# The opening of an FFT and gated MLP kernel: order of its transfers, z tiles of two chunks, the first weight quarter ahead of x

## The chip, the cores and the metric

The kernel runs on one core of one Trainium2 chip. The metric is device time in microseconds (us) of one execution; lower is better.

## The reference

x has the shape (8, 3008, 256): 8 batches of 3008 rows. The output has 24064 rows of 256 columns. All is fp32. Cut to what matters:

```python
X = np.fft.fft(np.fft.fft(x, axis=1), axis=2).real      # the transform
h = X.reshape(8 * 3008, 256) @ w_in                     # 256 -> 2048
g = h * np.cos(h)
out = g @ w_out                                         # 2048 -> 256
```

## The kernel before

**The transform.** A column of 3008 = 47 * 64 values is transformed in two halves. The first half (`first_half`) multiplies chunks of x by a constant L; its results are called z. The second half (`second_half`) multiplies z by a constant BJ, after z has been turned around: each chunk's z is copied from PSUM to SBUF by ScalarE (`keep_z`), stored to a scratch tensor in HBM (`store_z`, tensor zd), and loaded back in another layout (`load_z`, tile z). The transform along the 256 columns is not made on x: it is folded into the weights. `weights(e, n)` multiplies quarter n of moe_w_in (512 of 2048 columns) by the constant CS, with e = 0 for WC (cosine) and e = 1 for WS (sine); `keep_weights` copies the product to SBUF, and `fold_weights` does both. Row 0 of WS is used on its own: `take_wn(0)` turns it into per-partition scalars wn by four tiny products, and for the other quarters `send_wn(n)` stores the row to HBM (tensor wd) and `load_wn(n)` loads it back as a column of wn. GpSimd clears the row after that.

**Batches, chunks, groups.** A batch has 32 pairs of x rows' residues, cut into 8 chunks of 4 (`first_half(b, c)`, c = 0 to 7). x is loaded in 4 pieces of two chunks each (`load_x(b, p)`): four transfers for a piece, and six for piece 0. `fold(b, c, e)` prepares a chunk (VectorE and GpSimd for batch 0, GpSimd later). The second half has 6 groups (`second_half(b, g)`), each of 225 or 256 columns of tokens.

**The main loop.** For each batch and group there are 8 steps, one for each pair of feature blocks, and each step has two half-steps; k counts the half-steps over all. In a half-step TensorE multiplies the group by WC and WS (`mm1`, line 550), ScalarE and VectorE compute h * cos(h) (lines 562 to 592), GpSimd forms sums (line 608), and TensorE multiplies by moe_w_out and combinations of it (`mm2`, line 641; the combinations come from `combine_w2` on GpSimd). `seed` (line 531) writes the start value of an `mm1` sum and needs the wn column of that feature block, so quarter n of wn is wanted from k = 4 n - 1 on. The transform of batch b + 1 is spread over the loop of batch b (`transform`).

**The opening** is the code ahead of the loop: the transform of batch 0 as far as the first group, the first weights, and all loads of constants. Its order is written out by hand, and every engine works through its own instructions in that order. Transfers are issued by SP (`nc.sync`), except for some by ScalarE (`nc.scalar`). `keep_busy` runs products whose results nobody reads. In the opening each `store_z` stores the part of z that group 0 needs (j 0 to 4); the rest (j 4 to 24) is stored and loaded later.

**Order before.** SP's list: L, piece 0 of x, CS, weight quarter 0, pieces 1 to 3 of x, weight quarter 1, a piece of BJ (line 207), weight quarter 2; then the stores of z chunk by chunk, the loads of z, the first part of moe_w_out, weight quarter 3, and so on. Chunks 4 to 7 are stored by ScalarE. TensorE: first halves 0 and 1, the weights of quarter 0, first halves 2 to 7, three more weight products (quarter 1 twice, quarter 2 once), the second half of group 0, `keep_busy`, the loop. The remaining three weight products are made in the loop's first half-steps (`pw`, line 893 and 930).

Buffers: z chunks lie in tiles of 512 columns; tags "zs" (4 buffers) and, for chunks 4 to 7 of batch 0, "pq". The raw weight quarters 0 to 2 lie in two tiles under the tags "mr" and "cb", quarter 3 under "r"; these tags are used otherwise in the loop.

Of the kernel before, what the change touches and what calls it, by code (L numbers as in the profile page):

```python
# [114 lines left out]
def kernel(  # L115
# [30 lines left out]
    def load_x(b, p):  # L146
        if (b, p) not in xs:
            take_x(b, p)
        xt = xs[b, p]
        xv = xt.rearrange("r (i d) -> r i d", d=ND)  # L150
        i0 = XP * p
        for r0, r1, at, by in ((0, 32, 0, 3), (31, 47, 2, 6)):
            lo, hi = xv[at:NX:by], xv[at + by // 2 : NX : by]
            nc.sync.dma_start(out=lo, in_=x_r[b, r0:r1, i0 : i0 + XP, :])  # L154
            if p == 0:
                nc.sync.dma_start(out=hi[:, 0:1], in_=x_r[b, r0:r1, 32:33, :])  # L156
                nc.sync.dma_start(  # L157
                    out=hi[:, 1:XP], in_=x_r[b, r0:r1, 63 : 64 - XP : -1, :]
                )
            else:  # L160
                nc.sync.dma_start(
                    out=hi, in_=x_r[b, r0:r1, 64 - i0 : 64 - i0 - XP : -1, :]
                )
# [3 lines left out]
    wr = [spool.tile([128, 7 * 256], FP, tag=tag, bufs=1, name="wr") for tag in ("mr", "cb")]  # L167
    wl = spool.tile([128, 1024], FP, tag="r", bufs=4, name="wr")

    def raw(q, i):  # L170
        return wl[:, 512 * i : 512 * i + 512] if q == 3 else wr[i][:, 512 * q : 512 * q + 512]
# [5 lines left out]
    def load_cs():  # L177
        for i in range(2):
            nc.sync.dma_start(out=CS[i], in_=CS_dr.ap()[i * 128 : (i + 1) * 128, :])

    def load_w(q):
        for i in range(2):
            nc.sync.dma_start(
                out=raw(q, i),
                in_=moe_w_in[i * 128 : (i + 1) * 128, 512 * q : 512 * q + 512],
            )
# [12 lines left out]

    nc.sync.dma_start(out=L, in_=L_dr.ap())  # L200
    load_x(0, 0)
    load_cs()
    load_w(0)
    for p in (1, 2, 3):
        load_x(0, p)
    load_w(1)
    load_bj(0, 512)
    load_w(2)
# [51 lines left out]
    zss = {}  # L260

# [36 lines left out]
    def keep_z(b, c, pz):  # L298
        tag, n = ("zs", 4) if b or c < 4 else ("pq", 8)
        zs = spool.tile([128, 512], FP, tag=tag, bufs=n, name="zs")  # L300
        nc.scalar.copy(out=zs, in_=pz)
        zss[b, c] = zs
# [32 lines left out]
    def store_z(b, c, j0=0, j1=NJ, eng=nc.sync):  # L335
        half, q = divmod(c, NCH // 2)
        if q == 0 and j0 == 0:
            zds[b, half] = dpool.tile([32, 2 * NJ * 128], FP, tag="zd", bufs=4, name="zd")
        zd, zs = zds[b, half], zss[b, c]
        for e in range(2):  # L340
            p0 = 16 * e + IP * q
            eng.dma_start(
                out=zd[p0 : p0 + IP, 256 * j0 : 256 * j1].rearrange("i (y d) -> y i d", d=128),
                in_=zs[64 * e + 2 * j0 : 64 * e + 2 * j1, :].rearrange("y (i d) -> y i d", d=128),
            )

    def load_z(b, half, j0=0, j1=NJ):
        if b not in z2s:
            z2s[b] = spool.tile([128, NJ * 128], FP, tag="z2", bufs=1, name="z2")
        for r in range(2):  # L350
            p0 = 64 * half + 32 * r
            nc.sync.dma_start(
                out=z2s[b][p0 : p0 + 32, 128 * j0 : 128 * j1].rearrange("i (j d) -> i j d", d=128),
                in_=zds[b, half].rearrange("i (j r d) -> r i j d", r=2, d=128)[r, :, j0:j1],
            )
# [48 lines left out]
    def transform(b):  # L404
# [5 lines left out]
        for p in range(4):  # L410
# [5 lines left out]
            for c in (2 * p, 2 * p + 1):  # L416
                at(8 * p + 12, store_z, b, c)
# [9 lines left out]
    def fold_weights(e, n, tag="M"):  # L427
        keep_weights(e, n, weights(e, n, tag))

    def weights(e, n, tag="M"):  # L430
        pw = psum("pw", tag)
        for i in range(2):
# [351 lines left out]
    def chunk(c):  # L784
        fold(0, c, 0)
        fold(0, c, 1)

    keep_busy(2, "H", 512)
    keep_busy(2, "H", 512)
    chunk(0)  # L790
    chunk(1)
    first_half(0, 0)
    chunk(2)
    first_half(0, 1)
# [3 lines left out]
    store_z(0, 0, 0, 4)  # L798
    store_z(0, 1, 0, 4)
    chunk(3)  # L800
    first_half(0, 2)
    chunk(4)
    first_half(0, 3)
    store_z(0, 2, 0, 4)
    store_z(0, 3, 0, 4)
    chunk(5)
    first_half(0, 4)
    chunk(6)
    first_half(0, 5)
    store_z(0, 4, 0, 4, nc.scalar)  # L810
    store_z(0, 5, 0, 4, nc.scalar)
    load_z(0, 0, 0, 4)
    chunk(7)
    first_half(0, 6)
    store_z(0, 6, 0, 4, nc.scalar)
    first_half(0, 7)
    store_z(0, 7, 0, 4, nc.scalar)
    load_z(0, 1, 0, 4)
    fold_weights(1, 1)
    send_wn(1)  # L820
    fold_weights(0, 1)
    fold_weights(1, 2)
    send_wn(2)
    load_w2(0, 2)
    load_w(3)
    load_w2(2, 4)
    load_wn(1)
    load_wn(2)
    for c in range(8):
        store_z(0, c, 4)  # L830
# [39 lines left out]
    keep_busy(2, "M", 256)  # L870
    steps[0].pq, steps[0].nb = ready[0, 0]
    for k in range(2 * n + LAG):
# [5 lines left out]
        if cur:  # L878
# [13 lines left out]
            if k == 0:  # L892
                pw = [weights(1, 3)]
# [50 lines left out]
        if k in (1, 2, 3):  # L944
            e, q = ((1, 3), (0, 3), (0, 2))[k - 1]
            keep_weights(e, q, pw[k - 1], nc.vector.tensor_copy)
# [49 lines left out]
```

## Time and profile before

| what | value |
|---|---|
| median of 3 runs | 1946.1 us (1945.9 to 1946.29) |
| profiled execution | 1945.75 us |
| its span, first to last instruction | 1944.0 us |
| TensorE (PE) busy | 1934.2 us, 99% of the span |
| share of PE in the chain that ended last | 98% |
| first product of the main loop (line 550) | starts at 32.30 us |
| transfers | 89.10 MB, mean 46 GB/s; 12.78 MB of it in the first 60 us, 213 GB/s |

All engines run beside each other. PE is the matrix unit, PEld its weight loads, DVE is VectorE, ACT is ScalarE, POOL is GpSimd, SP issues transfers. A time in the trace is counted from the first instruction. An fp32 product shows as two passes on PE, so a count of x4 is two products. The chain that ended last is followed from the last instruction back to whatever released each step. "Idle before" an instruction is the time for which its engine did nothing, and the name behind the arrow is what ended that.

### The profile page before, as it was taken

The page shows a single profiled execution, that of the slowest core. Times are in us where ns is not written, and L with a number is a line of the kernel's source. Part 1 is how long each engine was busy: PE and PEld are TensorE (multiplying, and loading weights), DVE is VectorE, ACT ScalarE, POOL GpSimd, SP SyncE. Part 2 cuts the span into 40 slices and gives each one's busy share as a digit, 9 for nine tenths or more (in the row PEclk, how much of TensorE's full clock was granted, in tenths as well). Part 3 has the DMA queues.
Part 4 walks back from the last instruction along what each step waited for, and adds up shares of the span by engine and source line. Part 5 has one row for each costly group of instructions (what it writes and reads, how often), then busy time and mean ns, then how long its engine had stood idle before and what let it go on. Part 6 is the DMA issues. An engine that isn't in the chain of part 4 may idle for free.

```text
span 1944.0 us, 29626 instructions
## 1 busy us (share of the span) xinstructions
PE 1934.2 (99%) x9234; PEld 1681.9 (87%) x9234; DVE 1459.2 (75%) x2532; ACT 1508.4 (78%) x3444; POOL 1398.0 (72%) x1594
## 2 busy tenths in 40 slices
PE   9999999999999999999999999999999999999998
PEld 5888898888988889888898888988889888898887
DVE  4777777777777777777777777777777777788787
ACT  4777778777787787878778787788777887778775
POOL 3777767786677766787668776677767777666765
PEclk9999999999999999999999999999999999999999
DMA  7511122021220223111130111311013111100001
GB/s 201 129 29 39 35 53 71 18 40 40 57 58 18 42 43 80 32 24 40 40 90 21 39 25 41 88 24 40 22 42 88 24 39 28 39 23 16 11 14 31
DMA packets 178494, 89.10 MB, mean 46 GB/s; under 512 B 104945, under 2 KB 175391, under 8 KB 176674
## 3 DMA queue, kind: packets, MB, share of 16 engines
q1 hardware_dynamic: 176636, 86.68, 19.2%
q8 instruction: 75, 1.23, 0.3%
q10 hardware_dynamic: 1702, 0.53, 0.1%
q14 instruction: 81, 0.66, 0.1%
HBM read 49.90 MB, written 37.28 MB: 45 GB/s over the span
## 4 chain that ended last, share of the span: by engine, by line
PE 98%; DMA 1%; SPq 0%; DVE 0%; ACT 0%; issue 0%; POOL 0%; POOLq 0%; DVEq 0%
PE M L641 58%; PE H L550 33%; PE pz L275 3%; PE pb L366 2%; DMA wn<-wd 1%; DMA xp<-in_x_dram 1%; PE pw L433 1%; PE pz L272 0%; SPq L154 0%; PE pm L323 0%; DVE r L582 0%; ACT r L588 0%; DVE cb L709 0%; SPq L157 0%; SPq L156 0%
## 5 line engine op out<-in xcount | busy, mean ns | idle before, releaser
L608 POOL TENSOR_TENSOR S<-r 128x512 f32<-128x512 f32 (+1 forms) x383 | 475.0, 1240 | 445.5 <-DVE r L592 396.6
L582 DVE SCALAR_TENSOR_TENSOR r<-r,H 128x512 f32<-128x512 f32 (+1 forms) x768 | 518.8, 675 | 194.6 <-ACT r L578 167.9
L588 ACT ACTIVATE r<-r 128x512 f32<-128x512 f32 (+1 forms) x768 | 477.0, 621 | 240.5 <-DVE r L582 235.6
L592 DVE SCALAR_TENSOR_TENSOR r<-H,r 128x512 f32<-128x512 f32 (+1 forms) x768 | 519.1, 676 | 131.1 <-ACT r L588 90.6
L641 PE MATMUL M<-S,VX 128*128 128x256 f32 (+1 forms) x2304 | 615.2, 376 | 0.0
L641 PEld LDWEIGHTS M<-S,VX 128*128 128x128 f32 x2304 | 435.4, 190 | 71.3 <-issue 22.7
L550 PE MATMUL H<-pq,WC 128*128 128x256 f32 (+1 forms) x1536 | 453.4, 377 | 0.4 <-ACT H L531 0.3
L550 PE MATMUL H<-pq,WS 128*128 128x256 f32 (+1 forms) x1536 | 451.1, 375 | 0.5 <-ACT ew L562 0.5
L578 ACT ACTIVATE r<-H 128x512 f32<-128x512 f32 (+1 forms) x768 | 447.7, 583 | 0.2 <-DVE H L566 0.2
L566 DVE TENSOR_TENSOR H<-ew,H 128x256 f32<-128x256 f32 (+1 forms) x768 | 324.8, 423 | 140.3 <-PE H L550 81.3
L641 PE MATMUL M<-r,w 128*128 128x256 f32 (+1 forms) x1536 | 387.7, 375 | 0.0
L562 ACT ACTIVATE ew<-H 128x256 f32<-128x256 f32 (+1 forms) x768 | 287.8, 375 | 120.2 <-PE H L550 115.9
L531 ACT ACTIVATE H<-nb,wn 128x256 f32<-128x256 f32 (+1 forms) x766 | 366.0, 478 | 2.3 <-DMA wn<-wd 1.4
L641 PEld LDWEIGHTS M<-r,w 128*128 128x128 f32 x1536 | 300.4, 196 | 27.1 <-DVE mr L666 0.2
L550 PEld LDWEIGHTS H<-pq,WS 128*128 128x128 f32 x1536 | 289.9, 190 | 34.5 <-issue 1.0
L550 PEld LDWEIGHTS H<-pq,WC 128*128 128x128 f32 x1536 | 279.2, 190 | 44.6 <-ACT H L531 9.3
L614 POOL TENSOR_TENSOR S<-S,r 128x256 f32<-128x256 f32 (+1 forms) x383 | 275.5, 719 | 30.0
L615 POOL TENSOR_TENSOR S<-r,S 128x256 f32<-128x256 f32 (+1 forms) x383 | 274.5, 717 | 30.0
L641 PE MATMUL M<-S,w 128*128 128x256 f32 (+1 forms) x768 | 225.2, 375 | 0.0
L641 PE MATMUL M<-r,VX 128*128 128x256 f32 (+1 forms) x768 | 225.1, 375 | 0.0
L641 PEld LDWEIGHTS M<-S,w 128*128 128x128 f32 x768 | 150.4, 196 | 14.6
L641 PEld LDWEIGHTS M<-r,VX 128*128 128x128 f32 x768 | 145.8, 190 | 14.6
(78 smaller groups left out, 918.3 us busy)
## 6 DMA issues: line engine op xcount, KB each, us to landing
out_dram<-ob SPq DMA_DIRECT2D x724, 32.0 KB
xp<-in_x_dram SPq DMA_DIRECT2D x56, 256.0 KB
zd<-zs SPq DMA_DIRECT2D x112, 96.0 KB
z<-zd SPq DMA_DIRECT2D x28, 384.0 KB
xp<-in_x_dram SPq DMA_DIRECT2D x56, 128.0 KB
nb<-nd SPq DMA_DIRECT2D x39, 128.0 KB
wr<-in_moe_w_in_dram SPq DMA_DIRECT2D x8, 256.0 KB
w<-in_moe_w_out_dram SPq DMA_DIRECT2D x4, 512.0 KB
```

The source lines that it names most:

```text
L531: nc.scalar.activation(out=h.H[:, 0:T], in_=s.nb[:, 0:T], func=AF.Copy, bias=0.25, scale=wn[:, f : f + 1])
L550: nc.tensor.matmul(h.H[:, 0:T], lhsT=W[:, 128 * f : 128 * f + 128], rhs=s.pq[:, e * T : e * T + T], start=False, stop=True, skip_group_che ...
L562: nc.scalar.mul(out=h.ew[:, 0:T], in_=h.H[:, 0:T], mul=2.0)
L566: nc.vector.tensor_tensor(out=h.H[:, T : 2 * T][:, ::-1], in0=h.ew[:, 0:T], in1=h.H[:, 0:T], op=ALU.subtract)
L578: nc.scalar.activation(out=r, in_=y, func=AF.Copy, bias=BIG, scale=1.0)
L582: nc.vector.scalar_tensor_tensor(out=r, in0=r, scalar=-BIG, in1=y, op0=ALU.add, op1=ALU.subtract)
L588: nc.scalar.activation(out=r, in_=r, func=AF.Sin, bias=0.0, scale=SIN_SCALE)
L592: nc.vector.scalar_tensor_tensor(out=r, in0=y, scalar=-0.25, in1=r, op0=ALU.add, op1=ALU.mult)
L608: tt(out=sv[:, 0:2], in0=qv[:, 1:2].to_broadcast([128, 2, T]), in1=qv[:, 0:4:3], op=ALU.subtract,)
L614: tt(out=sv[:, 2], in0=sv[:, 1], in1=gv[:, 0, 0], op=ALU.subtract)
L615: tt(out=sv[:, 3], in0=gv[:, 1, 0], in1=sv[:, 2], op=ALU.add)
L641: nc.tensor.matmul(acc[key][m // 2][:, 256 * (m % 2) : 256 * (m % 2) + T], lhsT=w, rhs=a, start=first, stop=s.fp == 7, skip_group_check=True,)
```

## The change

It touches the opening and the tiles of z:

- CS and weight quarter 0 are loaded first, half by SP and half by ScalarE. Then comes piece 1 of x (its second halves by ScalarE), then L, then pieces 0, 2 and 3.
- Weight quarters 1, 2 and 3 are one transfer each in place of two.
- z is kept in tiles of two chunks (1024 columns), and one `store_z` stores two chunks: half as many stores, in all batches. In batch 0 the z tiles of chunks 4 to 7 take buffers of x.
- TensorE begins with shorter `keep_busy` products, then the weights of quarter 0, then the first halves of chunks 2, 3, 0, 1, 4 to 7.
- Weight quarters 1 to 3 and the first part of moe_w_out are issued between the stores of z and ahead of the first load of z. The last store and the last load of the opening are split between SP and ScalarE.
- The three weight products ahead of the loop are copied by VectorE, not ScalarE.
- The `keep_busy` between the second half of group 0 and the loop gives way to the first half of a weight product of quarter 3; its second half stays in the loop's half-step 0.

```diff
--- before.py
+++ after.py
@@ -143,7 +143,7 @@
     def take_x(b, p):
         xs[b, p] = spool.tile([128, XP * ND], FP, tag="xp", bufs=4, name="xp")
 
-    def load_x(b, p):
+    def load_x(b, p, other=nc.sync):
         if (b, p) not in xs:
             take_x(b, p)
         xt = xs[b, p]
@@ -153,37 +153,42 @@
             lo, hi = xv[at:NX:by], xv[at + by // 2 : NX : by]
             nc.sync.dma_start(out=lo, in_=x_r[b, r0:r1, i0 : i0 + XP, :])
             if p == 0:
-                nc.sync.dma_start(out=hi[:, 0:1], in_=x_r[b, r0:r1, 32:33, :])
-                nc.sync.dma_start(
+                other.dma_start(
                     out=hi[:, 1:XP], in_=x_r[b, r0:r1, 63 : 64 - XP : -1, :]
                 )
+                other.dma_start(out=hi[:, 0:1], in_=x_r[b, r0:r1, 32:33, :])
             else:
-                nc.sync.dma_start(
+                other.dma_start(
                     out=hi, in_=x_r[b, r0:r1, 64 - i0 : 64 - i0 - XP : -1, :]
                 )
 
 
     CS = [cpool.tile([128, 256], FP, tag=f"CS{i}", name=f"CS{i}") for i in range(2)]
-    wr = [spool.tile([128, 7 * 256], FP, tag=tag, bufs=1, name="wr") for tag in ("mr", "cb")]
-    wl = spool.tile([128, 1024], FP, tag="r", bufs=4, name="wr")
+    wr = {
+        q: spool.tile([128, n], FP, tag=tag, bufs=m, name="wr")
+        for q, tag, n, m in ((0, "r", 1024, 4), (1, "mr", 1792, 1), (2, "cb", 1792, 1), (3, "r", 1024, 4))
+    }
 
     def raw(q, i):
-        return wl[:, 512 * i : 512 * i + 512] if q == 3 else wr[i][:, 512 * q : 512 * q + 512]
+        return wr[q][:, 512 * i : 512 * i + 512]
 
     L = cpool.tile([128, 256], FP, tag="L", name="L")
     BJ = cpool.tile([128, NJ * 128], FP, tag="BJ", name="BJ")
     w2 = cpool.tile([128, 16 * ND], FP, tag="w2", name="w2")
 
-    def load_cs():
-        for i in range(2):
-            nc.sync.dma_start(out=CS[i], in_=CS_dr.ap()[i * 128 : (i + 1) * 128, :])
+    def load_first():
+        for tiles, src, c0, c1 in (
+            (CS, CS_dr.ap(), 0, 256),
+            ([raw(0, i) for i in range(2)], moe_w_in, 0, 512),
+        ):
+            for i, eng in enumerate((nc.sync, nc.scalar)):
+                eng.dma_start(out=tiles[i], in_=src[i * 128 : (i + 1) * 128, c0:c1])
 
     def load_w(q):
-        for i in range(2):
-            nc.sync.dma_start(
-                out=raw(q, i),
-                in_=moe_w_in[i * 128 : (i + 1) * 128, 512 * q : 512 * q + 512],
-            )
+        nc.sync.dma_start(
+            out=wr[q][:, 0:1024].rearrange("p (i f) -> p i f", i=2),
+            in_=moe_w_in[:, 512 * q : 512 * q + 512].rearrange("(i p) f -> p i f", p=128),
+        )
 
     def load_bj(c0, c1):
         nc.sync.dma_start(out=BJ[:, c0:c1], in_=B_dr.ap()[:, c0:c1])
@@ -197,15 +202,11 @@
             in_=moe_w_out.rearrange("(q p) c -> p q c", p=128)[:, 2 * f0 : 2 * f1],
         )
 
+    load_first()
+    load_x(0, 1, nc.scalar)
     nc.sync.dma_start(out=L, in_=L_dr.ap())
-    load_x(0, 0)
-    load_cs()
-    load_w(0)
-    for p in (1, 2, 3):
+    for p in (0, 2, 3):
         load_x(0, p)
-    load_w(1)
-    load_bj(0, 512)
-    load_w(2)
     WC = cpool.tile([128, NDFF], FP, tag="WC", name="WC")
     WS = cpool.tile([128, NDFF], FP, tag="WS", name="WS")
     wn = cpool.tile([128, 16], FP, tag="wn", name="wn")
@@ -258,6 +259,7 @@
                 nc.gpsimd.tensor_copy(**ends)
 
     zss = {}
+    zps = {}
 
     def first_half(b, c, pz=None):
 
@@ -296,10 +298,14 @@
         keep_z(b, c, pz)
 
     def keep_z(b, c, pz):
-        tag, n = ("zs", 4) if b or c < 4 else ("pq", 8)
-        zs = spool.tile([128, 512], FP, tag=tag, bufs=n, name="zs")
-        nc.scalar.copy(out=zs, in_=pz)
-        zss[b, c] = zs
+        p, q = divmod(c, 2)
+        if (b, p) not in zps:
+            if b == 0 and p > 1:
+                zps[b, p] = spool.tile([128, XP * ND], FP, tag="xp", bufs=4, name="zs")
+            else:
+                zps[b, p] = spool.tile([128, 1024], FP, tag="zs", bufs=2, name="zs")
+        zss[b, c] = zps[b, p][:, 512 * q : 512 * q + 512]
+        nc.scalar.copy(out=zss[b, c], in_=pz)
 
     def patch_z(b, c):
         small.append(
@@ -332,24 +338,24 @@
     zds = {}
     z2s = {}
 
-    def store_z(b, c, j0=0, j1=NJ, eng=nc.sync):
-        half, q = divmod(c, NCH // 2)
-        if q == 0 and j0 == 0:
+    def store_z(b, p, j0=0, j1=NJ, engs=(nc.sync, nc.sync)):
+        half, q = divmod(p, 2)
+        if (b, half) not in zds:
             zds[b, half] = dpool.tile([32, 2 * NJ * 128], FP, tag="zd", bufs=4, name="zd")
-        zd, zs = zds[b, half], zss[b, c]
+        zd, zs = zds[b, half], zps[b, p][:, 0:1024]
         for e in range(2):
-            p0 = 16 * e + IP * q
-            eng.dma_start(
-                out=zd[p0 : p0 + IP, 256 * j0 : 256 * j1].rearrange("i (y d) -> y i d", d=128),
+            p0 = 16 * e + XP * q
+            engs[e].dma_start(
+                out=zd[p0 : p0 + XP, 256 * j0 : 256 * j1].rearrange("i (y d) -> y i d", d=128),
                 in_=zs[64 * e + 2 * j0 : 64 * e + 2 * j1, :].rearrange("y (i d) -> y i d", d=128),
             )
 
-    def load_z(b, half, j0=0, j1=NJ):
+    def load_z(b, half, j0=0, j1=NJ, engs=(nc.sync, nc.sync)):
         if b not in z2s:
             z2s[b] = spool.tile([128, NJ * 128], FP, tag="z2", bufs=1, name="z2")
         for r in range(2):
             p0 = 64 * half + 32 * r
-            nc.sync.dma_start(
+            engs[r].dma_start(
                 out=z2s[b][p0 : p0 + 32, 128 * j0 : 128 * j1].rearrange("i (j d) -> i j d", d=128),
                 in_=zds[b, half].rearrange("i (j r d) -> r i j d", r=2, d=128)[r, :, j0:j1],
             )
@@ -413,8 +419,7 @@
             for k in range(4):
                 at(8 * p + (6, 7, 9, 10)[k], fold, b, 2 * p + k // 2, k % 2)
             pairs[per * (b - 1) + 8 * p + 12] = b, 2 * p
-            for c in (2 * p, 2 * p + 1):
-                at(8 * p + 12, store_z, b, c)
+            at(8 * p + 12, store_z, b, p)
         middles.add(per * (b - 1) + 11)
         at(23, load_z, b, 0)
         at(39, load_z, b, 1)
@@ -424,12 +429,12 @@
 
 
 
-    def fold_weights(e, n, tag="M"):
-        keep_weights(e, n, weights(e, n, tag))
-
-    def weights(e, n, tag="M"):
-        pw = psum("pw", tag)
-        for i in range(2):
+    def fold_weights(e, n, tag="M", copy=nc.scalar.copy):
+        keep_weights(e, n, weights(e, n, tag), copy)
+
+    def weights(e, n, tag="M", pw=None, both=(0, 1)):
+        pw = pw or psum("pw", tag)
+        for i in both:
             nc.tensor.matmul(
                 pw,
                 lhsT=CS[i][:, 128 * e : 128 * e + 128],
@@ -785,49 +790,44 @@
         fold(0, c, 0)
         fold(0, c, 1)
 
-    keep_busy(2, "H", 512)
-    keep_busy(2, "H", 512)
-    chunk(0)
-    chunk(1)
-    first_half(0, 0)
-    chunk(2)
-    first_half(0, 1)
+    both = nc.sync, nc.scalar
+    copy_v = nc.vector.tensor_copy
+    keep_busy(1, "H", 512)
+    keep_busy(1, "H", 512)
+    keep_busy(1, "M", 128)
     fold_weights(1, 0, "H")
     fold_weights(0, 0, "H")
     take_wn(0)
-    store_z(0, 0, 0, 4)
-    store_z(0, 1, 0, 4)
-    chunk(3)
-    first_half(0, 2)
-    chunk(4)
-    first_half(0, 3)
-    store_z(0, 2, 0, 4)
-    store_z(0, 3, 0, 4)
-    chunk(5)
-    first_half(0, 4)
-    chunk(6)
-    first_half(0, 5)
-    store_z(0, 4, 0, 4, nc.scalar)
-    store_z(0, 5, 0, 4, nc.scalar)
+    for p in (1, 0):
+        for c in (2 * p, 2 * p + 1):
+            chunk(c)
+            first_half(0, c)
+        store_z(0, p, 0, 4)
+        if p:
+            load_w(1)
+            load_bj(0, 512)
+    load_w(2)
+    load_w(3)
+    load_w2(0, 2)
     load_z(0, 0, 0, 4)
-    chunk(7)
-    first_half(0, 6)
-    store_z(0, 6, 0, 4, nc.scalar)
-    first_half(0, 7)
-    store_z(0, 7, 0, 4, nc.scalar)
-    load_z(0, 1, 0, 4)
-    fold_weights(1, 1)
+    for p in (2, 3):
+        for c in (2 * p, 2 * p + 1):
+            chunk(c)
+            first_half(0, c)
+        store_z(0, p, 0, 4, both if p == 3 else (nc.sync, nc.sync))
+    load_z(0, 1, 0, 4, both)
+    fold_weights(1, 1, "M", copy_v)
     send_wn(1)
-    fold_weights(0, 1)
-    fold_weights(1, 2)
+    fold_weights(0, 1, "M", copy_v)
+    fold_weights(1, 2, "M", copy_v)
     send_wn(2)
-    load_w2(0, 2)
-    load_w(3)
     load_w2(2, 4)
+    store_z(0, 1, 4)
+    store_z(0, 0, 4)
     load_wn(1)
     load_wn(2)
-    for c in range(8):
-        store_z(0, c, 4)
+    store_z(0, 2, 4)
+    store_z(0, 3, 4)
     load_bj(512, 1024)
     for half in range(2):
         load_z(0, half, 4)
@@ -867,7 +867,7 @@
         h.H = psum("H", "H")
         nc.vector.memset(h.H[:, 0 : h.s.T], 0.25)
     second_half(0, 0)
-    keep_busy(2, "M", 256)
+    pw = [weights(1, 3, both=(0,))]
     steps[0].pq, steps[0].nb = ready[0, 0]
     for k in range(2 * n + LAG):
         t, u = divmod(k, 2)
@@ -890,7 +890,7 @@
             if k < AHEAD - 1:
                 mm1(cur, 1)
             if k == 0:
-                pw = [weights(1, 3)]
+                weights(1, 3, pw=pw[0], both=(1,))
         pair = None if u else pairs.pop(t, None)
         if pair:
             b, c = pair
@@ -943,7 +943,7 @@
             dve_h(cur)
         if k in (1, 2, 3):
             e, q = ((1, 3), (0, 3), (0, 2))[k - 1]
-            keep_weights(e, q, pw[k - 1], nc.vector.tensor_copy)
+            keep_weights(e, q, pw[k - 1], copy_v)
         if k == 3:
             send_wn(3)
         elif k == 6:
```

## The prediction

> **What bounds the kernel now.** I read the page first: the shares of the engines and of the chain that ended last.
>
> ```profile
> span 1944.0 us, 29626 instructions
> PE 1934.2 (99%) x9234; PEld 1681.9 (87%) x9234; DVE 1459.2 (75%) x2532; ACT 1508.4 (78%) x3444; POOL 1398.0 (72%) x1594
> PE 98%; DMA 1%; SPq 0%; DVE 0%; ACT 0%; issue 0%; POOL 0%; POOLq 0%; DVEq 0%
> ```
>
> PE is the chain, except in the opening. The change adds no PE work after the opening, so it can only move the moment at which the loop starts, take PE work out of the loop's start, or close gaps of PE. The chain cut to the first 80 us shows them (start, length, what):
>
> ```profile
> 14.58 5.94 DMA xp<-in_x_dram
> ...
> 24.31 5.36 PE pw L433 x12
> ...
> 29.69 0.59 ACT WS L444
> ...
> 30.35 1.13 PE pb L366 x8
> ...
> 32.34 0.60 PE H L550 x2
> ...
> 49.23 11.89 DMA wn<-wd
> ...
> 61.14 0.46 ACT H L531
> ```
>
> The last quarter of x lands at 20.52 (14.58 + 5.94). First halves follow, then three weight products (24.31 to 29.67), then pb, the second half of the first group, at 30.35; the loop's first products follow from 32.30. ACT's copy to WS is named as pb's releaser, but pb reads BJ and z: what came at the same moment is the last z load, whose issue ended at 28.77. So two paths meet at 30.3: PE's order and the way of z through memory. Later there is one stall, on wn's last quarter (issued 49.23, landed 61.12). PE's timeline (start, us, engine, line, form, count, idle time before):
>
> ```profile
> 1.45 6.06 PE L497 MATMUL pd<-VX 128*128 128x512 f32 x8 [1.45 <-DVE VX L488]
> 24.24 5.42 PE L433 MATMUL pw<-wr,CS 128*128 128x512 f32 x12
> 32.30 0.65 PE L550 MATMUL H<-pq,WC 128*128 128x225 f32 x2
> 35.46 1.88 PE L433 MATMUL pw<-wr,CS 128*128 128x512 f32 x4
> 60.69 0.69 PE L397 MATMUL pn<-pq,ones 1*128 1x256 f32 x2
> 61.64 0.65 PE L550 MATMUL H<-pq,WC 128*128 128x225 f32 x2 [0.26 <-ACT H L531]
> ```
>
> And from ACT's, the copy of the last chunk of z, which stood behind ACT's own stores:
>
> ```profile
> 25.33 0.59 ACT L301 COPY zs<-pz 128x512 f32<-128x512 f32 x1 [0.70 <-DMA zd<-zs]
> ```
>
> Last, the stretches (length, busy time of the engines, PEclk, share and GB/s of the DMA engines at the end of each row):
>
> ```profile
> 1.50:7.00 5.50, 5.50 (x8) 2.33 (x8) 0.02 (x1) 0.83 (x2) 1.07 (x2) 1.00 0.68 193
> 7.00:10.00 3.00, 2.55 (x17) 1.40 (x16) 2.48 (x4) 0.20 (x1) 1.31 (x2) 1.00 0.88 244
> 10.00:20.00 10.00, 9.59 (x41) 4.59 (x38) 4.81 (x8) 3.77 (x8) 3.05 (x5) 1.00 1.03 250
> 20.50:23.00 2.50, 2.37 (x12) 1.10 (x10) 2.36 (x4) 0.85 (x2) 1.23 (x2) 1.00 1.02 371
> 23.00:28.00 5.00, 5.00 (x18) 2.31 (x15) 0.60 (x3) 1.78 (x4) 0.00 (x0) 1.00 0.26 49
> ```
>
> The DMA engines are full from 10 to 23 us, underfed before 7, and nearly idle from 23 to 28.
>
> **x lands earlier.** Up to x's last quarter both kernels load the same 4.06 MB (L 0.13, CS 0.26, the first weight quarter 0.52, x 3.15), in another order. Before, 193 × 5.5 + 244 × 3 = 1.79 MB had moved by 10 us. SP alone issues there, 0.4 to 0.7 us a transfer, some of 16 or 32 KB. After, SP and ACT each issue 128 to 256 KB pieces at once. Fed at the full rate of 250 GB/s from 1.8 us, 2.05 MB have moved by 10 us: 0.26 MB, or 1.0 us ahead. Bounds: 0 (no better fed) and 2.0 (CS and weights, 0.79 MB, at 371 in place of 250 GB/s). I take 1.0, because x's own packets make the 250: x lands at 19.5.
>
> [...] With this term at 0 the sum below would be -1.8 in place of -2.8.
>
> **From x to pb, by PE.** Before, 20.52 to 24.31 held the folds of two chunks and the first halves behind them: 3.8 us, which stays. Three weight products stay too: 5.36. So PE is free at 19.5 + 3.8 + 5.4 = 28.7. Their copies go from ACT (0.59) to DVE (0.69 by its row at 38.06). DVE sat idle 12.01 us up to 35.66 before, which hides them; without that cover each costs 0.1 us. The first weight quarter moves from 10.77 on PE to about 5.3; x was the later input there, so nothing is gained or lost: from 5.3, 3.7 + 1.0 us of weights and four pairs of first halves at 2.85 (18.50 to 21.34 before) end at 21.4 if packed, 1.9 us before the 23.3 that x allows.
>
> **From x to pb, by z.** SP's list now has the weight quarters w1, w2, w3, a piece of BJ and the first quarter of moe_w_out (0.52 + 0.52 + 0.52 + 0.26 + 0.52 = 2.36 MB, to which I count the z of the other pairs, 0.33) ahead of the last pair's stores. That is the price: before, only 1.3 MB stood there. By 20.52, 4.48 MB had moved (1.79 + 2.50 by 20.00, then 0.52 us at 371), so 0.42 of the 2.36 travel beside x. Left are 1.94 MB and the z: 2.27 / 0.371 = 6.1 us, and 0.8 more because z's 512 byte pieces run at 170 GB/s (the row of 36 to 43 us): 19.5 + 6.9 = 26.4. The last store lands 0.6 later (27.0, an estimate from the 1.6 that it took before in empty queues, last issue at 26.3, load behind it freed at 27.9); the z load is issued by SP and ACT side by side at 27.1 and takes 1.9 as before (its last issue began at 28.35, pb at 30.3): pb at 29.0. Bounds: 27.6 (nothing queued: the copy of the last chunk at 23.95, a store of 1.6, a load of 1.9; PE's 28.7 then decides) and 32.0 (the rest at 250 GB/s). I stay at 371 because it is the row of such weight pieces. SP's first z load also waits, for the first two pairs' stores behind w1 and BJ, to some 21.5; behind it are the third pair's stores, ready at about 21: inside the time in which the weights hold the queue. The removed waits of ACT (2.09 and 0.70 us idle on its own stores ahead of the last two copies) are in that sum. pb moves from 30.35 to 29.0: **-1.35**. On ACT, its half of the load stands ahead of both sends of wn and of pq's copies; it waits till 27.1 and frees ACT long before pq's copies at 30.2. The second send waits for DVE at 29.4 and costs 0.24 us: still ahead of them.
>
> **Half a weight product out of the loop.** Between pb and the loop PE ran four filler passes (31.32, 0.86 us) while ACT copied pq. Two passes of the fourth weight quarter (0.43 each, half of the 1.72 at 35.46) stand there now, and the loop's first unit has 0.86 less. PE ran without a gap from 32.30 to 43.07, so all of it counts: **-0.86**. Bounds: -0.4 (DVE's fraction ends 0.4 us after the earlier product, and it could become the limit) and -0.86.
>
> **The stall on wn.** PE's row at 60.69 is two passes of some 0.2 us, so PE was ready at about 61.07 and went on at 61.64: 0.6 lost. w3 and w2's first part (1.05 MB) now move in the idle stretch 23 to 28, so the big constants that the wn load lay among end 3 to 4 us earlier, against 2.2 for the loop. The margin is then over 1 us: **-0.6**, bounds 0 and -0.6. Late next: POOL. It clears a row of WS once the second send has landed (34.82 before), then runs eight combinations of 0.72 us, and had 1.00 us idle before the first sums. The send is issued 0.7 earlier, the loop runs 2.2 earlier: 1.5 of slack goes, 1.0 + 1.6 (sums end at 44.72, PE wants them at 46.32) are there. Cost 0, at most 0.5.
>
> **At nothing:** halved stores in later batches carry the same bytes off the chain (PE covers them; without it, SP's issue of some 0.35 us each would be the saving); the z tiles in x's buffers make the third and fourth loads of the next batch wait for stores that end some 10 us sooner, and SP's output stores queue behind those; if the stores were late, these would wait as well. ACT's four early issues (0.6 each) delay its table load to about 3 us, hidden since its first copy comes after 7.
>
> **Sum:** -1.35 - 0.86 - 0.6 = -2.8. The profiled execution took 1945.75 (span 1944.0 and 1.75 around it); so span 1941.2, execution 1942.95. The median of the runs shown is 1946.1, 0.35 above it: 1943.3. A measurement of this kernel can tell about 0.2% (3.9 us) from no change, so this is within it.
>
> **Rivals.** *More gain (0.20):* x lands 2.0 earlier and z is not held up: PE then sets pb at 27.7, -2.65 - 0.86 - 0.6 = -4.1, or 1942.0. For it: 371 GB/s in 20.5 to 23; against it: 250 wherever x moves. *Weights in front of z (0.10):* the 2.27 MB run at 250, pb at 32.0: +1.65 - 1.46 = +0.2, or 1946.3. For it: only 193 to 250 outside one stretch. *Half-speed PE (0.08), slower:* the filler at the start falls from 8 passes of 512 columns to 4 and 2 of 128, 1.45 to about 5.2. Weight loads of the filler followed each other at 0.85 us up to 5.88 and at 0.43 after, though PEclk reads 1.00. If the first weight quarter comes late and PE stays at the slow pace through it and four first halves, 3.7 + 1.0 + 5.7 = 10.4 us of work take twice that. The margin of 1.9 is the point from which it decides; the other 8.5 fall on PE's 28.7: pb at 37.2, so +6.85 - 1.46 = +5.4, or 1951.5. Against it: a gap of 0.45 us at 7.5 left the fast pace alone, and I see none over 2 us.
>
> [...]
>
> **Numbers.** Forecast 0.62, others as above. The range leaves out the slow clock and the best of the gains: 1941.0 to 1946.1. Faster 0.24 (the first rival and the forecast's edge), same 0.67, slower 0.09.
>
> **What would show it.** x's last fold waits till 19.5 in place of 20.5; pb at 29.0, after a z load, not after weights; mm1 at 31.0; no ACT idle on wn near 59. Wrong if passes of pw after 6.5 us start over 0.5 apart, if z's last store lands after 28, or if a new gap of PE shows between 31 and 60.

## The result: slower by 0.33%, and the profile after

The median of the changed kernel is 1952.3 us (1950.7 to 1955.5) against 1946.1: a ratio of 1.0033, 95% interval [1.0021, 1.0044]. The forecast was 1943.3, with a range that ended at 1946.1. The profiled execution took 1955.4 us, with a span of 1953.6, 9.6 more than before. (It is one of the longer runs of this kernel: over its seven runs the mean granted clock goes from 0.998 to 0.995 as the time goes from 1950.7 to 1955.5. So medians and profiled executions are told apart below.)

The page first: the span, the engines, and the shares of the chain.

```profile
span 1953.6 us, 29500 instructions
PE 1938.5 (99%) x9228; PEld 1684.5 (86%) x9228; DVE 1460.9 (75%) x2535; ACT 1507.2 (77%) x3441; POOL 1397.2 (72%) x1594
PE 98%; DMA 1%; SPq 0%; DVE 0%; ACT 0%; issue 0%; ACTq 0%; POOL 0%; POOLq 0%; DVEq 0%
```

PE is busy 4.3 us longer with six instructions fewer: the same work took longer. The other 5.3 us are idle time. The chain of the first 60 us shows where (start, length, what):

```profile
1.66 7.76 DMA xp<-in_x_dram
9.44 0.51 SPq L154
...
15.85 4.30 DMA xp<-in_x_dram
...
24.59 5.30 DMA zd<-zs
29.96 1.80 DMA zd<-zs
31.91 2.30 DMA z<-zd
...
34.46 2.05 PE pb L372 x8
36.51 1.71 PE pw L438 x2
```

x's last quarter landed at 20.15, against 20.52 before. PE was through the first halves at 23.9 and through the three weight products at 29.3. But the last pair of z stores, ready at 24.6, landed at 29.89 (ACT's part) and at 31.76 (SP's part, issued only at 29.96). The z load could not go before 31.91, and pb started at 34.46, 4.11 later than before. What SP's own list waited for, in us, times, and longest:

```profile
SPq L348 <- DMA zd<-zs: 4.3, 1, 4.3
SPq L154 <- DMA xp<-in_x_dram: 2.4, 1, 2.4
```

The first row is SP's half of the last store standing behind ACT's half. The second is early: SP's list of x pieces stood 2.4 us, until 9.44, behind a piece of x that ACT had issued. Both are inferred from what landed as the wait ended.

PE's timeline has the pause, and what followed it:

```profile
12.39 2.00 PE L277 MATMUL pz<-xf,L 128*64 128x512 f32 x5 [1.73 <-POOL xf L259]
23.87 5.42 PE L438 MATMUL pw<-wr,CS 128*128 128x512 f32 x12
34.46 2.05 PE L372 MATMUL pb<-BJ,z 128*128 128x128 f32 x8 [5.18 <-DMA z<-zd]
36.30 1.92 PE L438 MATMUL pw<-wr,CS 128*128 128x512 f32 x2
38.01 0.96 PE L555 MATMUL H<-pq,WC 128*128 128x225 f32 x2
```

PE stood still for 5.18 us; in the opening of before its longest idle time, once it ran, was 0.70. The same eight passes of pb then took 2.05 us in place of 1.13, and two passes of a weight product 1.92 where the four of before took 1.88. The stretches say the same (length, PE's busy time, PEclk, share and GB/s of the DMA engines):

```profile
10.00:15.00 5.00, 3.27 (x16) 0.83 0.85 214
20.15:25.00 4.85, 4.65 (x20) 1.00 0.94 292
25.00:30.00 5.00, 4.29 (x10) 1.00 0.63 202
30.00:34.40 4.40, 0.00 (x0) 0.92 0.26 57
34.40:40.00 5.60, 5.54 (x15) 0.50 0.80 219
40.00:45.00 5.00, 5.00 (x11) 0.50 0.75 213
49.00:52.00 3.00, 3.00 (x13) 1.00 1.19 187
```

PEclk is 0.50 from pb to beyond 45, and 1.00 again in the row from 49 on. It was also down near 13 us (0.50 from 13.25 to 16.67), behind the pause of 1.73 us in the first PE row above. That cost little here: PE waited 0.20 us for x's last quarter afterwards.

**Where 9.6 us went, in the profiled execution.** ACT's first instruction of a half-step (ew, line 567, 562 before) comes 9.21 us later than before from the fourth half-step on. Of that pb's start is 4.11, and the half weight product takes 0.86 back (shown below), so the low clock cost 9.21 - 4.11 + 0.86 = 5.96. From the thirteenth half-step on the shift is 8.88: 0.33 is won at wn. It grows again by 0.34 near 1004 us and 0.2 near 1675, and 0.2 more after the last of them: 9.6.

### The profile page after: what moved, and what is told of

Its sections match the earlier page's. It is cut to its first block, busy times and chain, and to the rows that moved or that the text cites. A ratio compares the mean times of both kernels' runs of the same rounds, so it can differ in the third digit from the quotient of the medians.

```text
span 1953.6 us, 29500 instructions
## 1 busy us (share of the span) xinstructions
PE 1938.5 (99%) x9228; PEld 1684.5 (86%) x9228; DVE 1460.9 (75%) x2535; ACT 1507.2 (77%) x3441; POOL 1397.2 (72%) x1594
## 3 DMA queue, kind: packets, MB, share of 16 engines
q10 hardware_dynamic: 2302, 1.29, 0.3%
## 4 chain that ended last, share of the span: by engine, by line
PE 98%; DMA 1%; SPq 0%; DVE 0%; ACT 0%; issue 0%; ACTq 0%; POOL 0%; POOLq 0%; DVEq 0%
PE M L646 58%; PE H L555 34%; PE pz L277 3%; PE pb L372 2%; DMA xp<-in_x_dram 1%; DMA zd<-zs 0%; PE pw L438 0%; SPq L154 0%; PE pz L274 0%; PE pm L329 0%; DMA z<-zd 0%; PE H L542 0%; SPq L161 0%; DVE cb L714 0%; PE pn L403 0%
```

## The experiments

Theory: the weights that SP now issues ahead of the last z stores hold up the stores and so the z load; PE then pauses, and the pause brings the low clock. The kernel before, measured beside the kernels below, lay at 1946.0 to 1946.3. The first four experiments undo one cause each.

**Filler over the pause.**

```diff
+    keep_busy(6, "M", 512)
     second_half(0, 0)
```

> The changed kernel with six more products of 512 columns that nobody reads (12 passes, 5.2 us) on PE between the last weight product and pb, where PE sat idle 5.18 us. Nothing else moves. Theory of the clock: the pause itself costs 4.1 us (pb at 34.5 in place of 30.35) and a second cost comes on top, because PE runs at half pace after it (pb 2.05 us in place of 1.13, PEclk 0.50 from 34.4 to 47). With the filler pb stays at 34.4 to 34.7, takes 1.1 us, PEclk stays 1.00, the first act_e of half-step 4 comes near 47.2 in place of 52.3, and the median is 1949 (1948 to 1950), with a narrower spread than the 1950.7 to 1955.5 of the changed kernel. Rival: the slow stretch has another cause (the shorter filler at the start, or the products' order): then the pace of pb stays at 2 us and the median at 1952. Second rival: the slow stretch is hidden anyway because ACT and DVE set the pace of the first half-steps: pb is quick, but the median stays within 1 us of 1952.

Measured: 1949.9, ratio 1.0021 [1.0012, 1.0030]; runs of 1949.3 to 1951.0, where after had 1950.7 to 1955.5. PE's timeline:

```profile
28.77 5.31 PE L502 MATMUL pd<-VX 128*128 128x512 f32 x12
34.88 1.13 PE L372 MATMUL pb<-BJ,z 128*128 128x128 f32 x8 [0.80 <-DMA z<-zd]
35.85 1.02 PE L438 MATMUL pw<-wr,CS 128*128 128x512 f32 x2
```

pb is even 0.4 later than in after, yet takes 1.13 again, and PEclk is 1.00 throughout. The fifth half-step comes 5.5 us sooner than in after (46.77 against 52.30). So in after the pause cost its own length and, on top, a low clock: 5 us in these two profiled executions, 2.4 in the medians. The late z itself is untouched by filler. Another 0.7 is lost up to the ninth half-step, where ACT waits for a send of wn that landed after 6.74 us (46.77 to 53.51); so too, by 1.2, in the kernel below with moe_w_out's quarter alone moved.

**All of the last store by SP** (the two halves no longer wait for each other).

```diff
-        store_z(0, p, 0, 4, both if p == 3 else (nc.sync, nc.sync))
+        store_z(0, p, 0, 4)
```

> The changed kernel with both stores of the last pair of chunks issued by SP, none by ACT. Theory of the shared completion: SP's last store was ready at 24.6 but issued at 29.96, because it waited for ACT's store of the same chunks, which had been issued at 24.59 and landed at 29.89. With both on SP they are issued at 24.7 to 25.9, land behind the weights by about 28.5, and pb starts at 30.5 to 31.5; PE's pause shrinks to 1 to 2 us, PE stays at full pace, median 1945.5 (1944.5 to 1947). Rival, the queue of weights alone: any store issued at 24.6 lands near 29.9 behind what SP has queued; then pb is at 32.2, the pause 3 us, and the median 1947 to 1951 depending on whether the pause still slows PE. Rival, ACT's half of the z load is at fault: then nothing moves.

Measured: 1952.4, ratio 1.0028 [1.0016, 1.0040], as after. The chain:

```profile
26.16 4.88 DMA zd<-zs
```

The last store was issued 3.8 us sooner than SP's half in after (26.16 in place of 29.96) and landed only 0.7 sooner, at 31.05; pb at 33.80 after a pause of 4.79, again at the low clock (PEclk 0.50 from 34 to 40 us). The waiting of one half on the other is real, but it cost no more than 0.7 us: without it the store takes 4.88 us in place of 1.80.

**The weights behind the z load**, both of them, and then only the later one.

```diff
     load_w(2)
-    load_w(3)
-    load_w2(0, 2)
     load_z(0, 0, 0, 4)
...
     load_z(0, 1, 0, 4, both)
+    load_w(3)
+    load_w2(0, 2)
```

> The changed kernel with the fourth weight quarter and the first quarter of moe_w_out (1.05 MB) issued behind the last z load of the opening, not ahead of the first. Theory of the queue: the last stores then have only weight quarter 3 of 4 ahead of them, all landed by 25; both land at 26.3, pb starts at 28.8 to 29.5, right behind PE's weights (29.3), with no pause. The half product that fills the gap before the loop must then wait for its weight quarter, which lands about 32: the loop starts at 32.5 to 33 with a pause of 1.5 to 2.5 us, no slow clock; median 1945 to 1946.5. Theory that ACT's queue alone makes a store late: ACT's store still lands about 29.9, SP's last store waits for it, and pb stays near 34, median about 1952.

> The changed kernel with only the first quarter of moe_w_out (0.52 MB, 1.5 us at 350 GB/s) issued behind the last z load; the fourth weight quarter stays ahead. [...] If the price grows faster than the bytes (pieces of 1 KB hold the queue longer than those of 2 KB), ACT's store lands at 26.5 and pb is at 30.5 with no slow clock: 1945.5. Theory that ACT's queue alone makes a store late: nothing moves, 1952.

Measured: 1949.6 with both moved, ratio 1.0015 [1.0005, 1.0024], runs of 1945.6 to 1953.5; 1947.7 with only moe_w_out's quarter moved, 1.0007 [0.9999, 1.0016]. Both profiled executions are free of the low clock behind pb (1946.1 and 1946.9; PEclk 1.00 from 20 to 60 us). PE's rows of the first, then of the second:

```profile
29.88 1.13 PE L372 MATMUL pb<-BJ,z 128*128 128x128 f32 x8 [0.28 <-issue]
32.30 1.10 PE L438 MATMUL pw<-wr,CS 128*128 128x512 f32 x2 [1.29 <-DMA wr<-in_moe_w_in_dram]
```

```profile
30.89 1.13 PE L372 MATMUL pb<-BJ,z 128*128 128x128 f32 x8 [1.63 <-DMA z<-zd]
```

With neither of the two ahead of the last stores, these land within 2.2 us (24.91 to 27.15) and pb is at 29.88, 4.6 sooner than in after. With w3 alone ahead of them, it is 2.8 us and 30.89. The queue theory holds. But with both moved the half weight product waits 1.29 us for w3, so there is no gain. And six of its eleven runs lie at 1949.6 and above, with a mean clock of 0.995 to 0.997 where the others have 0.998 to 1.0: in some executions the clock was still lowered, and the profiled one does not show where.

**The other direction: the kernel before with this one step alone.** Its w3 and its first quarter of moe_w_out are issued ahead of the first z load.

```diff
     store_z(0, 5, 0, 4, nc.scalar)
+    load_w(3)
+    load_w2(0, 2)
     load_z(0, 0, 0, 4)
...
     send_wn(2)
-    load_w2(0, 2)
-    load_w(3)
```

> The kernel before, with one step of the change alone: the fourth weight quarter and the first quarter of moe_w_out (1.05 MB) are issued ahead of its first z load instead of behind the second one. Everything else (x's order, the long start filler, single-chunk stores, no half product) is the kernel before. My theory: those transfers hold up the last z stores and the z load, and nothing else of the change is needed for the loss: pb from 30.35 to between 32 and 34, with a pause of PE of 2.3 to 4.5 us ahead of it; if the pause is over 2.5 us, PEclk falls under 1.00 for 3 to 14 us after it; median 1948.5 to 1952. Rival: the loss needs the other parts too (larger stores, the late x of two queues, z load split over two queues); then pb stays within 0.8 us of 30.35, PEclk stays 1.00, and the median is 1945.5 to 1947.

Measured: 1952.1, ratio 1.0031 [1.0019, 1.0043]: the whole loss of the change, without the rest of it. PE's timeline and the stretches of this kernel:

```profile
24.92 5.42 PE L433 MATMUL pw<-wr,CS 128*128 128x512 f32 x12
35.81 2.05 PE L366 MATMUL pb<-BJ,z 128*128 128x128 f32 x8 [5.47 <-DMA z<-zd]
37.65 1.82 PE L497 MATMUL pd<-VX 128*128 128x256 f32 x4
```

```profile
30.00:35.00 5.00, 0.34 (x1) 0.74 0.92 251
35.00:40.00 5.00, 4.19 (x15) 0.58 0.69 164
40.00:45.00 5.00, 5.00 (x19) 1.00 0.69 186
```

The pause is 5.47 us, 1 more than I gave it, because here z's four loads queue behind 1.05 MB as well (issued from 28.09; the last took 4.87 us and landed at 35.7, where after's took 2.30). The clock is low from 32.4 to 39.2, within the 3 to 14 us expected; the 2.5 us from which I expected it was a guess, and no run shows such a limit.

**What else brings the low clock?** I tried the short filler at the start as the cause of the spread: with the weights moved as above, the start filler of before (first diff), and then also w3 put between the last stores and the z load, to bring it in for the half product (second diff).

```diff
-    keep_busy(1, "H", 512)
-    keep_busy(1, "H", 512)
-    keep_busy(1, "M", 128)
+    keep_busy(2, "H", 512)
+    keep_busy(2, "H", 512)
```

```diff
+    load_w(3)
     load_z(0, 1, 0, 4, both)
-    load_w(3)
     load_w2(0, 2)
```

> The kernel of e3_weights_behind with the long filler at the start put back (8 passes of 512 columns in place of 4 and 2 of 128); nothing else. In e3 the profiled execution was clean (1946.07, PEclk 1.00 after the start) but the runs went from 1945.6 to 1953.5 with mean clocks of 0.995 to 1.0. Theory of the clock, second place: with the short filler PE reaches its full pace late or loses it in the thin work between 5 and 17 us, in some runs and not in others; the long filler reaches to about 7.5, the weights to 11, the first halves follow without a pause. Then the runs lie within 1945.3 to 1947, median 1946. Rival: the pause before the half product (1.3 us, waiting for its weights) or the wait for pb costs the clock, and the start has no part: spread and median stay (1949.6).

> As e5_long_start, but the fourth weight quarter is issued right behind the last stores of z and ahead of the last z load, in the time in which SP waits for these stores to land; the first quarter of moe_w_out follows the load. Theory of the queue: the stores still land at 26.5 to 27, the weight quarter's 0.52 MB run by 28, the load lands at 29 to 29.6; pb at 29.9 as in e3, no pause behind it, mm1 at 31.6 to 32.0, half-step 4 at 42.1 (1.0 ahead of before), then 0.3 more where the wait on wn was. Median 1944.6 (1944.0 to 1945.6), under before's 1946.0. Rival: any 0.5 MB between a store and its load delays the load by its own 1.4 us and more; then pb is at 31 to 32, median 1946 to 1947.

Measured: 1951.2, 1.0021 [1.0011, 1.0031] and 1948.4, 1.0015 [1.0007, 1.0024]. My theory of the start fell: the spread stays (1946.5 to 1953.2), and PEclk still drops near 13 us in the profile (0.81 from 10 to 15 us). And 0.5 MB between store and load is enough to make z late: the z load took 4.3 us, where it took 2.4 with only moe_w_out's quarter moved. The second kernel's row and stretch (the row names the transfer behind it, but pb reads z):

```profile
31.80 1.13 PE L372 MATMUL pb<-BJ,z 128*128 128x128 f32 x8 [2.54 <-DMA w<-in_moe_w_out_dram]
```

```profile
34.00:40.00 6.00, 6.00 (x18) 0.73 0.74 181
```

PEclk is 0.73 in this stretch. But it fell only at 36.8, 5 us after the pause of 2.54 us had ended, with PE busy all the time between and pb at full pace. So it is not shown that this pause brought it down.

**x by one queue, and no half product.** Both start from the kernel just shown.

```diff
-    load_x(0, 1, nc.scalar)
+    load_x(0, 1)
```

```diff
-    pw = [weights(1, 3, both=(0,))]
+    keep_busy(2, "M", 256)
```

> As e6_w3_in_gap, but the first piece of x is loaded by SP alone; ACT issues only its halves of CS and of the first weight quarter. In the changed kernel SP's list stood still for 2.4 us (7.0 to 9.44) behind ACT's piece of x, and the DMA engines moved only 214 GB/s from 10 to 15 us; x landed at 20.15, only 0.37 before the 20.52 of before. If that halt cost the missing 0.6 us, x lands at 19.3 to 19.7 here, PE is free 0.5 to 0.8 earlier, and the median is 0.5 lower than e6. If issue by two queues gains nothing anywhere, x lands at 20.5 or later and the median is 0.3 higher.

> As e6_w3_in_gap, but the filler between pb and the loop is put back and the product of the fourth weight quarter is whole again in half-step 0. The term of the prediction: 0.86 us, since PE has no gap from the loop's start to half-step 4. So half-step 4's act_e comes 0.86 later than in e6 with pb at the same time, and the median is 0.8 to 0.9 higher. Rival: the first half-steps wait for ACT and DVE anyway, so the half product is hidden: difference under 0.4.

Measured: 1947.7, 1.0006 [0.9997, 1.0015] and 1951.2, 1.0028 [1.0017, 1.0039]. With x by SP alone the three weight products start 1.33 sooner in the profiled execution (23.84 in the kernel it starts from), and pb 1.9 sooner:

```profile
22.51 5.42 PE L438 MATMUL pw<-wr,CS 128*128 128x512 f32 x12
29.92 1.13 PE L372 MATMUL pb<-BJ,z 128*128 128x128 f32 x8 [1.99 <-DMA w<-in_moe_w_out_dram]
```

The DMA engines moved 260 GB/s from 10 to 15 us there, against 219 in the kernel it starts from. But this does not show two queues for x to be a loss of 1.33 us. The kernel it starts from had the low clock from 12.9 to 16.3, and this one had not; the first kernel of the next group, with x by SP alone and the same low clock, started these products at 23.83. The intervals of the two medians overlap too. The kernel without the half product is confounded: its code up to pb is the same, yet in its profiled execution z came late (pb at 33.49 after a pause of 3.50), and PEclk fell to 0.55 in the stretch from 34 to 40. Its time says nothing on the half product.

**The causes taken away together:** w3 and moe_w_out's quarter behind the z load, x by SP alone, the long start filler, no half product. Then two passes of filler more at 12 us (after take_wn(0)), and last the half product put back.

```diff
     take_wn(0)
+    keep_busy(1, "M", 512)
```

> The changed kernel with four steps of it taken back: the fourth weight quarter and the first quarter of moe_w_out go behind the last z load (as in e3), the first piece of x is loaded by SP alone (as in e7), the long filler at the start, and the whole product of the fourth weight quarter in half-step 0 with the filler before the loop. What stays of the change: CS and the first weight quarter ahead of x by two queues, z tiles of two chunks, the last store and load of z by two queues, the order of the pieces. Theory: x lands at 18.8 to 19.0 (e7), the last stores find an empty queue and land at 25.3, the z load at 27.5, just before PE is through with its weights (27.9 to 28.2): pb at 28.0 to 28.5 in place of 30.35, no pause over 1.3 us, no slow clock. Half-step 4's act_e at 40.8 to 41.2 (before: 43.09), 0.3 more where the wait on wn was: median 1943.6 (1943.0 to 1944.6), spread under 2 us. Rival: the slow clock comes from the pause of 1.26 us before the first of the first halves, or from any thin stretch of the opening: then the spread stays at 5 us and more and the median is over 1946. Rival: the z load cannot land before 29.5 whatever is queued: median 1945 or more.

> As e9_clear_way, with one more product of 512 columns (0.86 us) that nobody reads ahead of the first first-half, where PE sat idle 1.26 us in e5 to e7, in some profiles with PEclk below 1.00 right after. If that pause is what sets off the slow stretch at 13 us, this one shows PEclk 1.00 from 10 to 20 us in every profile and a narrower spread than e9, median 0 to 1 lower. If pauses of 1.3 us do nothing, it is the same as e9 within 0.3.

> As e10_clear_way_fill, with the half product of the fourth weight quarter back between pb and the loop. Its weights are issued behind the last z load (25.9) and land at 28.5 to 29.5, pb ends at 29.2: little or no wait. Then the term of the prediction holds alone: half-step 4 is 0.86 earlier than in e10 and the median 0.6 to 0.9 lower, 1942.9. Rival: the weights land at 30.5 or later, as in e3 (32.2, 2.3 us after pb's start): then the half product gives its gain back as a pause and the median is level with e10 or up to 1 us above it.

Measured: 1945.5, 0.9992 [0.9983, 1.0001]; 1945.3, 0.9994 [0.9985, 1.0002]; and 1945.6, 1.0003 [0.9995, 1.0011]. The loss in the median is gone; none is measurably faster than before. With the filler at 12 us PEclk was 1.00 from 10 to 15 us (0.79 in the first kernel), but the runs spread no less: 1943.5 to 1947.0, against 1943.3 to 1946.0. With the half product four of twelve runs lie at 1948.7 to 1951.1, with a mean clock of 0.997 to 0.998: there the low clock is not gone. PE's rows of the second and the third:

```profile
23.31 5.42 PE L438 MATMUL pw<-wr,CS 128*128 128x512 f32 x12
29.04 1.13 PE L372 MATMUL pb<-BJ,z 128*128 128x128 f32 x8 [0.31 <-DMA z<-zd]
30.99 0.65 PE L555 MATMUL H<-pq,WC 128*128 128x225 f32 x2
```

```profile
28.81 1.13 PE L372 MATMUL pb<-BJ,z 128*128 128x128 f32 x8 [1.10 <-DMA z<-zd]
31.05 1.10 PE L438 MATMUL pw<-wr,CS 128*128 128x512 f32 x2 [1.11 <-DMA wr<-in_moe_w_in_dram]
31.98 0.54 PE L555 MATMUL H<-pq,WC 128*128 128x225 f32 x2
```

In the second pb stands at 29.0, where the forecast had it, and the loop starts 1.31 sooner than before. (In the first, with the low clock near 13 us, pb came at 29.94.) The half product then costs what it saves (0.86): it waits 1.11 us for w3, which is issued behind z. In none of the orders tried did both z and w3 come early.

## Why the prediction was wrong

**The step that failed** is "From x to pb, by z": "2.27 / 0.371 = 6.1 us" and "The last store lands 0.6 later (27.0 ...)". The amount held: 292 GB/s over 4.85 us and 202 over 5.00 make 2.43 MB by 30.0. The DMA engines of after from 20 to 30 us, in forty slices of 0.25 us (busy share in tenths, then GB/s):

```profile
DMA  9998999899998897689999999999998421211100
GB/s 311 319 311 303 385 316 283 295 320 393 332 365 266 234 221 221 164 238 287 258 320 348 360 344 336 365 350 340 297 295 252 105 57 53 61 53 41 41 25 0
```

They were full to near 28.0, where the sum had its queue empty at 26.4: x was 0.65 later than forecast, and the 2.34 MB up to 28.0 moved at 299 GB/s, not 371. That is only 1.6 us of the 5.46 by which pb missed 29.0. The larger part came behind the queue. ACT's half of the last store, issued at 24.59, had its first packet moved at 26.96 and landed at 29.89, 1.9 us after 28.0 and not 0.6. SP's half came 1.87 after that, at 31.76, and from there to pb it was 2.7 and not 2.0. So the step took the time for the queue and then two store times on top, one behind the other, each nearly as long as one takes with neither of the two weights ahead (2.2 us). My lower rate, 250, gave 32.0 as the bound for pb; it came at 34.46. (The 0.8 us for z's short pieces is a slip besides: 0.33 MB at 170 in place of 371 GB/s are 1.05.) The kernel before with this step alone shows that nothing else is needed for the loss.

**The half-speed rival** had the mechanism, but at another place and by another sum: that its 1951.5 is near the median of 1952.3 is luck. I put it at the start filler, where a PEclk of 0.83 from 10 to 20 us did cost little, since x was later than PE. I set it at 0.08 because "I see none over 2 us", which was true of before only. My own bounds had pb at 32.0 with PE free at 28.7: a pause of 3.3 us made by the change, which I never put to that rival.

Pauses ahead of pb of 0.28 to 1.99 us left PEclk at 1.00 right behind them in the profiled executions; with 3.50, 4.79, 5.18 and 5.47 it was 0.55, 0.50, 0.50 and 0.58 in the stretch that begins about pb's start. But near 13 us it fell in seven traces, after among them, behind pauses as short as 1.73 us (after) and 1.26 (the long start filler, and w3 in the gap), while the kernel with x by SP alone had the same 1.26 there and stayed at 1.00 from 10 to 20. And runs of that kernel, whose pause ahead of pb was 1.99, reach 1950.9 at a mean clock of 0.997. So the runs show no length of pause that is safe.

**The other terms.** x earlier by 1.0: it was 0.37. By 10 us 2.04 MB had moved, as forecast (2.05); the lead was lost from 10 to 15, at 214 GB/s against 258 before. The second queue brought nothing there: from 10 to 15 us the kernels with x by two queues moved 185 to 219 GB/s, those by one 238 to 261. In after SP's list stood 2.4 us behind a piece that ACT had issued. The half product, -0.86: right wherever w3 was there. With only moe_w_out's quarter moved, pb is +0.54 against before and the fifth half-step -0.32; with the filler +4.53 and +3.67; without a half product pb and that half-step shift alike (-1.31 both). wn, -0.6: what came was 0.33, in after as in the last kernels and in the one with the one step. POOL at 0 held. The stores and tiles of later batches were not at nothing: 0.54 us in after, near 1004 and 1675 us, and about 0.4 to 0.55 in the other kernels with the change, where before with the one step has nothing; I did not follow its cause. "pb at 29.0" was reached only with the weights out of the way, and "if z's last store lands after 28, or if a new gap of PE shows between 31 and 60" was the sign that came.

**Open:** why, with both weights behind the z load, about half of the runs still show a low mean clock, and with the half product back a third of them; and how much of the kernel's wide spread is that the DMA engines deliver z at other times from run to run (31.80 and 33.49 by the same code).

## What to carry to other kernels

Here the 1.05 MB issued ahead of the first load of z held up z, and with it the loop (pb 4.11 later in after, and 5.46 in before with this step alone); the second issuing engine did not bring its half of the last store past them (5.30 us, against 2.2 with the weights behind). So keep the queue empty around a round trip through memory, and issue bulk loads behind it. When a change can let TensorE wait, add a low clock after the wait to the price (in after's profiled execution 5.96 us for a wait of 5.18), or put filler there (with it pb took 1.13 us at a PEclk of 1.00). And join the late bound of one path to the early bound of the other: the pause between them is a cost of its own.

## What was not expected of the hardware

The low clock outlasted the pause. With the pauses of 3.50, 4.79, 5.18 and 5.47 us PE was at 0.50 for about 10.2, 13.7, 13.7 and 6.8 us in the profiled executions, so its length did not follow the pause's. In after PEclk fell at 13.25, was back at 16.67, fell at 33.73 and was back at 47.39; the other lengths are estimates from the mean PEclk of their stretches. Nor did the fall come at a fixed place: in after about 4.5 us into the pause, in before with the one step about 2.1 us into it, and without the half product about 1.1 us behind its end. What ended the low clock is not shown. Before with the one step ran four passes of filler behind pb and was back after 6.8 us, but the kernel without the half product ran four there too and took 10.2.

And ACT's 32 KB half of the last store, which took 2.2 us with the weights behind it, took 5.3 when ACT issued it beside SP's weights, though ACT had no other transfer under way.
